# The 64-row matmul of the first feed-forward layer runs over 128 rows, with one more copy of weights

## The chip, the cores and the metric

The kernel runs on one core of a Trainium2 chip. The metric is the device time of one execution in microseconds (us), as the median over repeated runs. The names of the engines are those of the profile: PE is the matrix engine and PEld its weight loads, DVE, ACT and POOL are the vector, scalar and general engines, SP issues all transfers (DMA).

## The reference, cut to what matters

The program is a recurrent attention (mLSTM) followed by a feed-forward layer with a layer norm, over 4 batches, 8 heads of width 40, 768 time steps, all in float32:

```
attn_out = _attn_ref(q, k, v, i_gate, f_gate, o_gate)      # (4, 8, 768, 40)
x = attn_out.transpose(0, 2, 1, 3).reshape(4, 768, 320)
xn = (x - mean(x)) / sqrt(var(x) + 1e-6) * g_ln            # over the last axis
out = x + maximum(xn @ w_ch1, 0) @ w_ch2                   # w_ch1: 320 x 1280, w_ch2: 1280 x 320
```

The change touches only the product `xn @ w_ch1`. Its inner dimension is 320, that is 128 + 128 + 64.

## The kernel before

**Tiling.** Time is cut into 6 chunks of 128 steps; a step `st` of the attention is one chunk of one batch (24 steps). Two steps make a pair of 256 rows, and the feed-forward runs once for each pair (12 units `u`). In a unit the 1280 hidden columns are taken in 5 blocks `f` of 256, each in two halves `i` of 128.

**Precision in two parts.** The products of the feed-forward take operands of type `F32R`, so each operand is split into a high part and the small rest, and three of the four products of parts are summed: high by high, low weights by high data, high weights by low data. `w1h`, `w1l` are the parts of `w_ch1`, `XH`, `XL` those of the normalised rows, `hh`, `hl` those of the hidden values.

**The third slice of the inner dimension** has only 64 rows, and the other 64 partitions are put to use: in `XH[:, 2]` partitions 0 to 63 hold the high part of the last 64 features, and partitions 64 to 127 hold the low part of the same 64 features (`emit_xl`, L596, writes it there; the transposed input has these 64 features twice). `w1h[:, 2]` holds the high weights in both halves of the partitions, so a single matmul over 128 rows gives high by high and high by low. The product of low weights with high data takes partitions 0 to 63 alone, in a matmul over 64 rows.

**One half of the first layer**, `mm1` (task `m1`, L603 to L615), is thus eight matmuls that add up in one place: two `w1h` by `XH`, two `w1l` by `XH` over 128 rows, one `w1l` by `XH` over 64 rows, two `w1h` by `XL`, and one `w1h` by `XH` over 128 rows (third slice). There are 12 x 5 x 2 = 120 such halves. After both halves of a block ACT makes `hh` (L619) and DVE makes `hl` (L625), and `mm2` (L639 to L641, six matmuls for each of two halves of the rows) adds them into the second layer's output. `emit_ob` (L645) adds the residual, and a transfer stores the result.

**Weights.** They come in as raw float32 pairs, are converted by tasks `cA` to `cL`, and the key `"r"` is the third slice: the conversion (L671 to L717) fills partitions 0 to 63 for the columns 0 to 639 and partitions 64 to 127 for the columns 640 to 1279. `copy_r` (L722) then copies a half of the columns into the other half of the partitions by a transfer on SP: twice for `w1h`, and once for `w1l` (columns 640 to 1279 into partitions 0 to 63).

**Order.** All engines run a fixed order, written by a planner (`Plan`): each task has an engine, a duration, the tasks that it follows, buffers that it takes and gives, and a rank; the engine takes the ready task of least rank. The ranks come from a table of parameters (`TUNE`) and a table of offsets by task name (`OFF`, with `cR.0` -15.3, `cR.1` -10.4, `cR.2` -32.3). The planner prices `m1` at 0.87 us. What it leaves is one order of instructions per engine; on the chip an engine waits in that order. SP's transfers wait in order too, so that a transfer behind one that waits for a buffer is late with it.

Of the kernel before, what the change touches and what calls it, by code (L numbers as in the profile page):

```python
# [37 lines left out]


class Plan:  # L40
    """Orders the program: every engine takes, among the tasks that are ready, the one of least rank."""

    LAT = 0.12
    WIN, SLEEP, WAKE = 3.413, 0.45, 0.72
# [5 lines left out]
    def add(self, key, eng, us, fn, after=(), take=(), give=(), rank=0.0, kind=0, size=0, start=0.0, seq=None, load=1.0):  # L50
        rank += OFF.get(".".join(str(k) for k in key), 0.0)
        self.tasks[key] = dict(
            key=key, eng=eng, us=us, fn=fn, after=[a for a in after if a], take=take, give=give, rank=rank, kind=kind,
            size=size, start=start, seq=seq, load=load,
        )
# [95 lines left out]
def mlstm_moe_kernel(  # L151
# [40 lines left out]
    w1h = const.tile([128, 3, FF], F32R)  # L192
    w1l = const.tile([128, 3, FF], F32R)
# [409 lines left out]
    def mm1(p, f, i):  # L603
        if i == 0:
            h1_t[p, f] = ps_1.tile([128, 2, 256], F32, tag="h", name="h")
        ps = h1_t[p, f]
        XH, XL = XH_t[p], XL_t[p]
        cs = slice((2 * f + i) * 128, (2 * f + i + 1) * 128)
        ops = [(w1h[:, k, cs], XH[:, k]) for k in range(2)]
        ops += [(w1l[:, k, cs], XH[:, k]) for k in range(2)]  # L610
        ops += [(w1l[0:64, 2, cs], XH[0:64, 2])]
        ops += [(w1h[:, k, cs], XL[:, k]) for k in range(2)]
        ops += [(w1h[:, 2, cs], XH[:, 2])]
        for n, (a, x) in enumerate(ops):
            nc.tensor.matmul(ps[:, i], a, x, start=(n == 0), stop=(n == len(ops) - 1))  # L615
# [42 lines left out]
    def load_w(key):  # L658
        if key == "r":
            wload(key, w1r, 640)  # L660
        elif key[0] == "a":
            wload(key, w1a[key[1]], 512)
        else:
            wload(key, w2[key[1]], 640)

    def conv_a(key):
        n = 512 if key[0] == "a" else 640
        raw = w_st.pop(key)[:, :n].bitcast(I32).rearrange("p (n two) -> p n two", two=2)
        lo, hi = raw[:, :, 0], raw[:, :, 1]
        t = stage_p.tile([128, 640], I32, tag="t", name="wt")[:, :n]  # L670
        nc.scalar.activation(out=t.bitcast(F32), in_=hi.bitcast(F32), func=AF.Abs)  # L671
        w_st["t", key] = (lo, hi, t)

    def conv_x(key, e):
        t = w_st["t", key][2].bitcast(F32)
        e.tensor_scalar(out=t, in0=t, scalar1=UMIN, scalar2=None, op0=ALU.max)

    def conv_t(key, i):
        lo, hi, t = w_st["t", key]
        if i == 0:  # L680
            nc.vector.tensor_scalar(
                out=t, in0=t, scalar1=3, scalar2=0x3FFFFFF8, op0=ALU.logical_shift_left, op1=ALU.bitwise_and
            )
        elif i == 1:
            nc.vector.scalar_tensor_tensor(
                out=t, in0=hi, scalar=-0x40000000, in1=t, op0=ALU.bitwise_and, op1=ALU.bitwise_or
            )
        else:
            nc.vector.scalar_tensor_tensor(
                out=lo, in0=lo, scalar=29, in1=t, op0=ALU.logical_shift_right, op1=ALU.bitwise_or  # L690
            )
            w_st["t", key] = lo.bitcast(F32)
# [24 lines left out]
            e.tensor_tensor(out=l, in0=tf[ps], in1=h.bitcast(F32), op=ALU.subtract)  # L717

    def copy_r(i):
        w, a, h = ((w1h, 0, 0), (w1h, 1, 1), (w1l, 1, 1))[i]  # L720
        cs = slice(640 * h, 640 * h + 640)
        nc.sync.dma_start(  # L722
            out=w[64 - 64 * a:128 - 64 * a, 2, cs].bitcast(F32), in_=w[64 * a:64 * a + 64, 2, cs].bitcast(F32)
        )
# [135 lines left out]
    def plan_conv(n):  # L860
        key = keys[n]
        f = (n - 1) // 2
        r = TUNE["c0"] + n if n < 2 else T0 + TUNE["cv"] + TUNE["cs"] * (n - 2)
        rl = (TUNE["wl0"], TUNE["wl1"])[n] if n < 2 else TUNE["wl"] + TUNE["ws"] * (n - 2)
        k = 0.8 if key[0] == "a" else 1.0
        add(("wl", n), "sp", 0.5, lambda: load_w(key), [], seq=("wl", n - 1) if n else None, take=["wraw"], rank=rl,
            size=655360 * k, start=rl)
        xe, le = TUNE["cx"][n], TUNE["cl"][n]
        sc = le == "p"
        add(("cA", n), "act", 0.53 if key[0] == "a" else 0.64, lambda: conv_a(key), [("wl", n)], seq=("cA", n - 1) if n else None, take=["t"],  # L870
            rank=r, start=TUNE["cst"] if n > 1 else 0.0)
        add(("cX", n), "pool" if xe == "p" else "dve", (1.8 if xe == "p" else 0.41) * k,
            lambda: conv_x(key, nc.gpsimd if xe == "p" else nc.vector), [("cA", n)], rank=r)
        for i, d in enumerate((0.42, 0.75, 0.75) if key[0] != "a" else (0.35, 0.61, 0.61)):
            add(("cT", n, i), "dve", d, lambda i=i: conv_t(key, i), [("cT", n, i - 1) if i else ("cX", n)],
                give=["t"] if i == 2 else [], rank=r)
        if key == "r":
            dh, dl = 1.25, 3.0 if sc else 1.47
        elif key[0] == "a":
            dh, dl = 0.53, 1.24 if sc else 0.61  # L880
        else:
            dh, dl = 0.64, 1.5 if sc else 0.74
        add(("cH", n), "act", dh, lambda: conv_h(key), [("cT", n, 2)], rank=r)
        add(("cL", n), "pool" if sc else "dve", dl, lambda: conv_l(key, nc.gpsimd if sc else nc.vector), [("cH", n)],
            give=["wraw"], rank=r)
        if n == 0:
            for i in range(3):
                add(("cR", i), "sp", 0.6, lambda i=i: copy_r(i), [("cL", 0)], rank=r + i, size=163840)

    def plan_unit(u):  # L890
        r = slot(u)
        k = TUNE["k"] if u < 2 else KF // 2

        def before(u, f, m):
            last = KF // 2 - 1
            if u > 1 or TUNE["k"] > last:
                t = (u, f - 1) if f else (u - 1, last) if u else None
            else:
                ks = TUNE["k"]
                seq = [(v, g) for h in ((0, ks), (ks, last + 1)) for v in range(2) for g in range(*h)]  # L900
                i = seq.index((u, f))
                t = seq[i - 1] if i else None
            return (f"m{m}", *t, 1) if t else None

        def rank(f):
            if u > 1:
                return r + 4 * f
            if f < k:
                return T0 + TUNE["RA"] * u + 4 * f
            return T0 + TUNE["RB"] + 4 * (f - k) + 4 * u * (KF // 2 - k)  # L910

        for f in range(KF // 2):
            r = rank(f)
            for i in range(2):
                add(("m1", u, f, i), "pe", 0.87, lambda f=f, i=i: mm1(u, f, i),
                    [("xl", 2 * u), ("xl", 2 * u + 1), ("cL", 1 + 2 * f), ("cR", 0 if f < 2 else 2),
                     ("m1", u, f, 0) if i else before(u, f, 1) if k < 5 or f else None],
                    seq=("m1", u - 1, 4, 1) if u and k == 5 and not f and not i else None,
                    take=[] if i else ["h"], give=["xt"] if i and f == KF // 2 - 1 else [], rank=r + i)
            add(("hh", u, f), "act", 0.48, lambda f=f: emit_hh(u, f), [("m1", u, f, 1)], take=["ht"], rank=r)  # L920
            add(("hl", u, f), "dve", 0.61, lambda f=f: emit_hl(u, f), [("hh", u, f)], give=["h"], rank=r)
            for j in range(2):
                add(("m2", u, f, j), "pe", 0.81, lambda f=f, j=j: mm2(u, f, j, k),
                    [("hl", u, f), ("cL", 2 + 2 * f), ("m2", u, f - 1, j) if f and k == 5 else None, ("m2", u, f, 0) if j else before(u, f, 2) if k < 5 else None],
                    take=[f"o{j}"] if f in (0, k) else [], give=["ht"] if j else [], rank=r + 6 + j)
                if f in (k - 1, KF // 2 - 1):
                    add(("ob", u, j, f), "dve", 0.41, lambda j=j: emit_ob(u, j), [("m2", u, f, j)], give=[f"o{j}"],
                        rank=r + 4)
        for j in range(2):
            add(("out", u, j), "sp", 0.5, lambda j=j: store(u, j),  # L930
                [("ob", u, j, KF // 2 - 1), ("ob", u, j, k - 1) if k < KF // 2 else None], give=["y"], rank=slot(u),
                size=163840)
# [108 lines left out]
```

## Time and profile before

| what | us |
|---|---|
| runs (three) | 480.77, 483.7, 489.62 |
| median | 483.7 |
| span of the profiled execution | 477.9 |
| PE busy in it | 440.4 (92%) |
| DVE, ACT, POOL busy | 230.4, 176.2, 159.5 |

The page of the profile gives the profiled execution's span, from its first to its last instruction, and no other time of it; the fastest of the three runs is 2.9 us above the span, the median 5.8. A matmul's busy time in the profile runs from its start to a modelled end and overlaps the next one's, so the step from one matmul's start to the next one's is read from starts. The granted clock is the TensorE clock as a share of the higher of its two levels (2.4 and 1.2 GHz), as a mean over a stretch.

### The profile page before, as it was taken

To read this page: it belongs to the slowest core of one execution; us is meant where nothing else is said; L and a number is where in the kernel's file an instruction comes from. 1 tells how busy PE (TensorE), PEld (TensorE's weight loads), DVE (VectorE), ACT (ScalarE), POOL (GpSimd) and SP (SyncE) were. 2 spreads that over 40 slices of the span, in tenths; PEclk is the share of its full clock that TensorE was granted. 3 is DMA by queue.
4 is the path that set the end of the run, shared out by engine and by line. 5 is a ranking of instruction groups with operands and counts; after the bars stand their busy time and mean duration, and the time that the engine had idled before them with its cause. 6 is when DMAs were issued, how large, how long until landed. Compare 5 with 4: busy or idle time off the path is not lost.

```text
span 477.9 us, 7347 instructions
## 1 busy us (share of the span) xinstructions
PE 440.4 (92%) x2704; PEld 386.5 (81%) x2706; DVE 230.4 (48%) x524; ACT 176.2 (37%) x438; POOL 159.5 (33%) x195
## 2 busy tenths in 40 slices
PE   8999998999789997699998799988979988999996
PEld 4886787889679886688997698977868977989885
DVE  2475869975164752544545325453463443433321
ACT  3356556751151343414443313244243334222200
POOL 1145449661341560613623433252250522100100
PEclk8555779899979999579999859999997998999999
DMA  8935757637845879425776743686465585000000
GB/s 241 291 103 148 233 148 256 163 93 207 190 124 145 235 206 213 122 80 169 194 198 162 183 126 110 161 237 184 130 194 167 132 259 118 1 0 29 0 29 27
DMA packets 52721, 71.82 MB, mean 150 GB/s; under 512 B 3330, under 2 KB 45862, under 8 KB 52686
## 3 DMA queue, kind: packets, MB, share of 16 engines
q1 hardware_dynamic: 52686, 71.36, 54.1%
q8 instruction: 21, 0.34, 0.3%
q14 instruction: 14, 0.11, 0.1%
HBM read 46.83 MB, written 4.12 MB: 107 GB/s over the span
## 4 chain that ended last, share of the span: by engine, by line
PE 61%; DMA 22%; DVE 7%; SPq 3%; POOL 2%; issue 2%; ACT 2%; POOLq 0%; DVEq 0%; ACTq 0%
PE h L615 25%; DMA w<-gsc 8%; PE Y L481 6%; PE o L639 5%; PE s L411 5%; PE o L641 5%; PE o L640 5%; PE kv L444 2%; DMA og<-in_og_dram 2%; DMA raw<-in_qk_dram 2%; DMA ks<-raw 2%; DMA qs<-hi 2%; DMA qs<-raw 2%; SPq L257 2%; DMA eg<-esc 2%
## 5 line engine op out<-in xcount | busy, mean ns | idle before, releaser
L615 PE MATMUL h<-xh,w1h 128*128 128x256 f32 x360 | 91.2, 312 | 0.0
L615 PE MATMUL h<-xh,w1l 128*128 128x256 f32 x360 | 89.4, 327 | 0.0
L639 PE MATMUL o<-w2h,hh 128*128 128x320 f32 x240 | 83.1, 346 | 6.6 <-ACT hh L619 5.4
L619 ACT ACTIVATE hh<-h 128x512 fp32r<-128x512 f32 x60 | 35.6, 594 | 136.0 <-PE h L615 124.4
L641 PE MATMUL o<-w2h,hl 128*128 128x320 f32 x240 | 77.3, 322 | 0.5 <-DVE hl L625 0.5
L640 PE MATMUL o<-w2l,hh 128*128 128x320 f32 x240 | 76.8, 320 | 0.0
L615 PEld LDWEIGHTS h<-xh,w1l 128*128 128x128 f32 x360 | 62.8, 200 | 16.6 <-issue 2.5
L625 DVE SCALAR_TENSOR_TENSOR hl<-h,hh 128x512 fp32r<-128x512 f32 x60 | 41.2, 687 | 63.0 <-ACT hh L619 62.8
L363 ACT ACTIVATE w<-w,ar_sb 128x128 f32<-128x128 f32 x176 | 55.0, 390 | 33.1 <-POOL w L339 32.9
L615 PEld LDWEIGHTS h<-xh,w1h 128*128 128x128 f32 x360 | 64.3, 204 | 0.6
L615 PE MATMUL h<-xl,w1h 128*128 128x256 f32 x240 | 63.6, 348 | 0.0
L481 PEld LDWEIGHTS Y<-tok,w 128*128 128x128 f32 x384 | 55.4, 216 | 1.5 <-POOL rstd L552 1.1
L481 PE MATMUL Y<-tok,w 128*128 128x42 f32 x384 | 53.9, 293 | 0.6 <-ACT xh L584 0.6
L639 PEld LDWEIGHTS o<-w2h,hh 128*128 128x128 f32 x240 | 48.0, 200 | 7.5 <-ACT hh L619 5.8
L615 PEld LDWEIGHTS h<-xl,w1h 128*128 128x128 f32 x240 | 37.9, 199 | 16.4 <-issue 2.2
L641 PEld LDWEIGHTS o<-w2h,hl 128*128 128x128 f32 x240 | 47.6, 198 | 1.5 <-DVE hl L625 1.5
L418 DVE TENSOR_TENSOR w<-s,w 128x512 f32<-128x512 f32 x48 | 33.0, 688 | 31.4 <-PE s L411 26.5
L640 PEld LDWEIGHTS o<-w2l,hh 128*128 128x128 f32 x240 | 47.8, 199 | 0.0
L411 PE MATMUL s<-qs,ks 120*128 120x128 f32 (+1 forms) x240 | 41.0, 305 | 3.9 <-DMA qs<-raw 2.0
L411 PEld LDWEIGHTS s<-qs,ks 120*128 120x128 f32 (+1 forms) x240 | 36.2, 217 | 8.4 <-issue 7.5
L514 POOL TENSOR_TENSOR ogr<-og,rec 128x320 f32<-128x320 f32 x24 | 18.8, 781 | 65.3 <-DVE rec L507 50.1
L248 POOL TENSOR_TENSOR raw<-raw,hi 120x768 f32<-120x768 f32 x18 | 33.0, 1837 | 14.9 <-ACT hi L243 14.9
(91 smaller groups left out, 518.2 us busy)
## 6 DMA issues: line engine op xcount, KB each, us to landing
w<-gsc SPq DMA_DIRECT2D x22, 512.0 KB
tok<-in_tok_dram SPq DMA_DIRECT2D x12, 698.0 KB
raw<-in_qk_dram SPq DMA_DIRECT2D x9, 720.0 KB
ks<-hi SPq DMA_DIRECT2D x36, 180.0 KB
qs<-hi SPq DMA_DIRECT2D x36, 180.0 KB
out_dram<-y SPq DMA_DIRECT2D x24, 160.0 KB
qn<-in_qn_dram SPq DMA_DIRECT2D x10, 360.0 KB
eg<-esc SPq DMA_DIRECT2D x30, 120.0 KB
```

Source lines behind the costliest of these rows:

```text
L248: nc.gpsimd.tensor_tensor(out=raw[:, :, j], in0=raw[:, :, j], in1=hi[:, :, j], op=ALU.subtract)
L363: nc.scalar.activation(out=w[:, h], in_=w[:, h], func=AF.Exp, bias=ar_sb[:, c, 0, hb:hb + 1])
L411: nc.tensor.matmul(ps[:, hh], ks[:, h], qs[:, h], start=True, stop=True)
L418: nc.vector.tensor_tensor(out=w[:, half * 4:half * 4 + 4], in0=s_t.pop((st, half)), in1=w[:, half * 4:half * 4 + 4], op=ALU.mult)
L481: nc.tensor.matmul(Y[:, h * VA:(h + 1) * VA], w[:, h], tok_t[p][:, j, h * VA:(h + 1) * VA], start=(c == 0), stop=(c == 0 or h == H - 1), s ...
L514: nc.gpsimd.tensor_tensor(out=ogr, in0=og_t[c][:, b].rearrange("p (h d) -> p h d", h=H), in1=rec.to_broadcast([128, H, D]), op=ALU.mult,)
L615: nc.tensor.matmul(ps[:, i], a, x, start=(n == 0), stop=(n == len(ops) - 1))
L619: nc.scalar.activation(out=hh, in_=h1_t[p, f], func=AF.Relu)
L625: nc.vector.scalar_tensor_tensor(out=hl.rearrange("p a t -> p (a t)"), in0=ps.rearrange("p a t -> p (a t)"), scalar=0.0, in1=hh.rearrange( ...
L639: nc.tensor.matmul(ps, hh[:, i, sl], w2h[:, ff], start=(ff in (0, 2 * cut)), stop=False)
L640: nc.tensor.matmul(ps, hh[:, i, sl], w2l[:, ff], start=False, stop=False)
L641: nc.tensor.matmul(ps, hl[:, i, sl], w2h[:, ff], start=False, stop=(ff in (2 * cut - 1, KF - 1)))
```

## The change

In `mm1` the fifth of the eight matmuls takes all 128 partitions of `w1l[:, 2]` and `XH[:, 2]` in place of partitions 0 to 63; it then adds the product of low weights and low data for the last 64 features too. For this `w1l[:, 2]` must hold the low weights in both halves of the partitions for all columns, so `copy_r` gets a fourth copy (`w1l`, columns 0 to 639, into partitions 64 to 127), and the copies are numbered anew. An `m1` task now names copy 1 or 3 (the `w1l` copy of its columns) as what it follows, where it named copy 0 or 2. The docstring of `Plan` is gone.

```diff
-        ops += [(w1l[0:64, 2, cs], XH[0:64, 2])]
+        ops += [(w1l[:, 2, cs], XH[:, 2])]
...
     def copy_r(i):
-        w, a, h = ((w1h, 0, 0), (w1h, 1, 1), (w1l, 1, 1))[i]
+        w, a, h = ((w1h, 0, 0), (w1l, 0, 0), (w1h, 1, 1), (w1l, 1, 1))[i]
...
-            for i in range(3):
+            for i in range(4):
                 add(("cR", i), "sp", 0.6, lambda i=i: copy_r(i), [("cL", 0)], rank=r + i, size=163840)
...
                 add(("m1", u, f, i), "pe", 0.87, lambda f=f, i=i: mm1(u, f, i),
-                    [("xl", 2 * u), ("xl", 2 * u + 1), ("cL", 1 + 2 * f), ("cR", 0 if f < 2 else 2),
+                    [("xl", 2 * u), ("xl", 2 * u + 1), ("cL", 1 + 2 * f), ("cR", 1 if f < 2 else 3),
```

## Rows read from the trace of the kernel before

**Rows 1.** The page: the span, the engines' busy time, and the shares of the chain that ended last.
```profile
span 477.9 us, 7347 instructions
...
PE 440.4 (92%) x2704; PEld 386.5 (81%) x2706; DVE 230.4 (48%) x524; ACT 176.2 (37%) x438; POOL 159.5 (33%) x195
...
PE 61%; DMA 22%; DVE 7%; SPq 3%; POOL 2%; issue 2%; ACT 2%; POOLq 0%; DVEq 0%; ACTq 0%
```

**Rows 2.** Busy time by stretch: the stretch, its length, busy time (and instructions) of each engine, the mean granted clock, the busy share of the DMA engines, GB/s. Three stretches from the first feed-forward matmul to the end, then the conversion of the weights.
```profile
53.00:90.00 37.00, 35.38 (x194) 31.17 (x193) 30.10 (x52) 21.97 (x50) 24.14 (x20) 0.77 0.66 191
90.00:396.00 306.00, 278.88 (x1800) 250.41 (x1799) 145.43 (x347) 111.11 (x277) 110.80 (x133) 0.92 0.63 169
396.00:477.90 81.90, 76.86 (x507) 68.43 (x505) 26.43 (x63) 17.48 (x44) 7.04 (x13) 0.99 0.09 27
...
65.00:90.00 25.00, 23.38 (x154) 21.54 (x153) 23.20 (x37) 17.57 (x42) 20.40 (x18) 0.90 0.67 200
```

**Rows 3.** The chain that ended last, by line, in the stretches 53 to 90, 90 to 396 and 396 to 478 us (the view cuts each line off at its end).
```profile
by line: PE h L615 27.2%; DVE wraw L689 8.1%; issue 5.6%; DVE wt L681 5.1%; PE Y L481 4.6%; PE Y L432 4.2%; PE o L639 4.1%; DVE wt L685 3.8%; PE o L640 3.7%; PE o L641 3.7%; DVE hl L625 3.5%; PE kv L444 3.4%; DVE w1l L717 3.2%; DVE xn L563 
...
by line: PE h L615 24.9%; DMA w<-gsc 12.6%; PE o L639 5.3%; PE Y L481 4.8%; PE o L641 4.6%; PE o L640 4.5%; PE s L411 3.6%; DMA og<-in_og_dram 3.3%; DMA raw<-in_qk_dram 3.1%; DMA ks<-raw 2.8%; DMA qs<-hi 2.8%; DMA qs<-raw 2.7%; SPq L257 2.7
...
by line: PE h L615 42.4%; PE o L639 10.3%; PE o L641 10.3%; PE o L640 9.8%; DMA out_dram<-y 8.9%; PE Y L481 6.0%; PE Y L432 2.6%; PE xT L578 1.6%; DVE y L645 1.2%; PE s L411 1.0%; DVE hl L625 0.9%; ACT hh L619 0.7%; DVE y L523 0.6%; issue 0
```

**Rows 4.** Groups of instructions by line and shape, of the matmuls and weight loads that take `w1l`, over 128 and over 64 rows: busy us, mean ns of one, idle time before.
```profile
L615 PE MATMUL h<-xh,w1l 128*128 128x256 f32 x240 | 50.0, 291 | 0.0
...
L615 PE MATMUL h<-xh,w1l 64*128 64x256 f32 x120 | 47.9, 399 | 0.0
...
L615 PEld LDWEIGHTS h<-xh,w1l 128*128 128x128 f32 x240 | 39.7, 203 | 0.0
...
L615 PEld LDWEIGHTS h<-xh,w1l 64*128 64x128 f32 x120 | 23.1, 193 | 16.6 <-issue 2.5 <-ACT wt L671 0.2
```

**Rows 5.** Instructions in order of time, of one half at the full clock (448.70 to 450.04) and the start of the next: start us, length us, engine, line; neighbours of one kind stand merged (x2, x3) or alone, by the window that was asked for, and come from several windows here. "64*128" is the 64-row matmul or load.
```profile
448.70 0.29 PE L615 MATMUL h<-xh,w1h 128*128 128x256 f32 x1
...
448.82 0.28 PE L615 MATMUL h<-xh,w1h 128*128 128x256 f32 x1
448.94 0.40 PE L615 MATMUL h<-xh,w1l 128*128 128x256 f32 x2
...
448.95 0.19 PEld L615 LDWEIGHTS h<-xh,w1l 128*128 128x128 f32 x1
...
449.06 0.59 PE L615 MATMUL h<-xh,w1l 128*128 128x256 f32 x2
449.27 0.18 PEld L615 LDWEIGHTS h<-xh,w1l 64*128 64x128 f32 x1
...
449.27 0.38 PE L615 MATMUL h<-xh,w1l 64*128 64x256 f32 x1
449.58 0.39 PE L615 MATMUL h<-xl,w1h 128*128 128x256 f32 x1
...
449.80 0.28 PE L615 MATMUL h<-xl,w1h 128*128 128x256 f32 x1
...
449.92 0.52 PE L615 MATMUL h<-xh,w1h 128*128 128x256 f32 x3
450.28 0.70 PE L615 MATMUL h<-xh,w1l 128*128 128x256 f32 x3
```

**Rows 6.** The same view of one half at half the clock (205.31 to 207.75), with the weight load of its 64-row matmul.
```profile
205.31 0.77 PE L615 MATMUL h<-xh,w1h 128*128 128x256 f32 x2
205.88 1.14 PE L615 MATMUL h<-xh,w1l 128*128 128x256 f32 x3
206.95 0.80 PE L615 MATMUL h<-xl,w1h 128*128 128x256 f32 x2
207.54 0.41 PE L615 MATMUL h<-xh,w1h 128*128 128x256 f32 x1
207.75 0.41 PE L444 MATMUL kv<-tok,kp 128*120 128x126 f32 x1
...
206.44 0.28 PEld L615 LDWEIGHTS h<-xh,w1l 64*128 64x128 f32 x1 [0.22 <-issue]
```

**Rows 7.** The same view where a half follows a transposition over 32 rows (`gT`), at the full clock.
```profile
299.12 0.24 PE L310 MATMUL gT<-id_sb,uu 32*128 32x32 f32 x1
299.29 0.50 PE L615 MATMUL h<-xh,w1h 128*128 128x256 f32 x2
```

**Rows 8.** A transfer on the chain that ended last (start us, length us, what), and the busy time (columns as in the first view by stretch above) around it.
```profile
117.02 11.90 DMA w<-gsc
...
117.00:131.00 14.00, 11.68 (x83) 10.43 (x82) 2.77 (x9) 1.74 (x7) 4.10 (x5) 1.00 0.85 201
```

**Rows 9.** Who waited for whom: waiting engine and line, for what, us in total, times, longest us (SP's own queue); and, in order of time, a matmul with the idle time before it and what ended that in brackets.
```profile
SPq L211 <- DMA qs<-raw: 7.1, 4, 2.3
...
133.37 0.63 PE L639 MATMUL o<-w2h,hh 128*128 128x320 f32 x1 [4.68 <-ACT hh L619]
```

**Rows 10.** SP's queue around the copies: start us, length us, line, what.
```profile
26.80 0.57 SPq L722 DMA_DIRECT2D w1l<-w1l  x1
...
28.05 1.13 SPq L722 DMA_DIRECT2D w1h<-w1h  x2
38.29 0.33 SPq L216 DMA_DIRECT2D tok<-in_tok_dram  x1
```

## The prediction

> **What bounds the kernel now.** I read the page first. PE is busy in 92% of the span and no other engine in half of it; the chain that ended last lies 61% on PE and 22% on transfers [rows 1]. An average over stages with different limits doesn't say what a PE saving is worth, so next came the busy time by stretch [rows 2]. Up to 53 us there is no feed-forward matmul. From 53 to 90 us the weights are converted, and in its later part DVE is busy in 23.20 of 25 us. From 90 to 396 us PE is busy in 278.9 of 306 us, and 0.63 of the DMA engines' time is taken. From 396 us on the transfers are nearly over (0.09), and PE has 76.9 of 81.9 us. Then the chain by the same stretches [rows 3]: the line of the first layer, L615, holds 27.2% of it in the first, 24.9% in the middle and 42.4% at the end. The reader is to see that the changed line is the largest part of the chain everywhere, but that in the middle transfers stand between its pieces.
>
> Last I looked at what the 64-row matmul costs. By the groups, a 64-row matmul lasts 399 ns and a 128-row one of the same operands 291 ns [rows 4], but ends are modelled and overlap, so the price is read from starts. In one half at the full clock [rows 5] the eight matmuls start at 448.70, 448.82, 448.94, 449.06, 449.27, 449.58, 449.80 and 449.92; from 449.92 to 450.28, the third start of the next half, lie three steps, 0.12 each. So the steps are 0.12, 0.12, 0.12, **0.21, 0.31, 0.22**, 0.12, 0.12: 1.34 us. The three long ones lie before the 64-row matmul, after it, and after the next. The weight loads say why: an ordinary load starts with the matmul ahead of it (449.06's at 448.95, beside the one of 448.94), while the 64-row matmul's load starts at 449.27, only with its own matmul. The array goes from 128 rows to 64 and back with nothing loaded in advance, and the step behind catches up. The same catching up is seen after another change of rows: behind a 32-row transposition the first two matmuls of a half take 0.50 us [rows 7], like the two `xl` ones here (449.58 to 449.80 plus a length of 0.28), where a half in plain order has 0.40.
>
> **The change part by part.** (1) With 128 rows all eight should step by 0.12. That saves 0.21 + 0.31 + 0.22 - 3 x 0.12 = **0.38 us for each half** at the full clock. At half the clock [rows 6] the plain step is 0.21 (207.54 to 207.75); from the third to the fifth start 0.56, to the sixth 0.51, to the eighth 0.59, so the long steps are 0.35, 0.51 and 0.38, and 0.61 us goes of 2.44. Bounds: if the third gap belongs to reading `XL` and stays, 0.28 remains; I take 0.38, since [rows 7] shows that gap without `XL`.
>
> (2) How much of it shortens the end? 120 halves save about 48 us of PE's time (120 x 0.38, and 0.23 more for the ten or so at half clock). On the chain alone: at the end 42.4% of 81.9 us is 34.7 us, 26 halves, **9.8 us**. In the middle 24.9% of 306 us is 76.2 us; a granted clock of 0.92 means that 0.16 of the time is at half, so 0.84 x 0.284 + 0.16 x 0.25 = 0.279 of it goes, **21.2 us** (about 50 halves). In the first stretch 10.1 us, of which 2.5 would go; I take nothing, because behind it DVE converts weights almost without pause and the next matmuls wait for those. The other 39 or so halves run beside transfers of the chain, as in the 11.90 us of `w` from 117.02, when DMA is 0.85 busy and moves 201 GB/s [rows 8]. Such a transfer isn't shortened by a faster PE, so there some 15 us become PE's wait.
>
> (3) The fourth copy. SP's issues of the three copies take 0.57 and 1.13 for two [rows 10]; a fourth is 0.57 us, its wait is the one that the first copy has already ended, and behind it stands the `tok` load, which isn't issued until 38.29. So nothing is delayed; the first feed-forward matmul is at 53. Without that cover it would cost 0.57 us and about 0.8 us for 160 KB (an estimate, at 201 GB/s). The copy that the first blocks now follow is issued over 20 us ahead of them. SP's transfers wait on a ring of earlier ones, which shifts by one; such waits are up to 2.3 us [rows 9]. Bounds 0 to 2.3, taken as 0.
>
> (4) The planner. It prices `m1` the same, so ranks move only for the copies: the offsets of `cR.0` to `cR.2` now meet other copies and `cR.3` has none. A pick elsewhere could flip through the copy's 0.6 us of SP time. No row prices that; the nearest is PE's wait of 4.68 us [rows 9], so up to 5 us either way, taken as 0, because SP stands waiting right behind the copies. The matmul reads more partitions, and those are written by the same tasks as before.
>
> (5) The sum: 9.8 + 21.2 = 31 us. The profiled span becomes 477.9 - 31 = 447. What lies around the span isn't listed; the fastest run is 2.9 and the median 5.8 us above it, which gives 450 to 453. **I forecast 451 us.** Of the middle, what is late next are the transfers and the waits behind them (`w`, then ACT's `hh`, before which PE stood 4.68 us).
>
> A rule against it: a 64-row load lasts 193 ns and a 128-row one 203 [rows 4]. The Trainium skill, TensorE: Matmul & The Clock Gate, section LDWEIGHTS (loading the stationary operand), says that a load over 32 rows takes as long as one over 128, as only columns count; the trace agrees. By that rule alone the rows matter nowhere and the sum is 0.
>
> **The rivals.** A, the forecast, 443 to 462 us: the chain's share is saved, with an error of some 10 us for its clock and its transfers. 0.62.
>
> B, all of PE's time is saved: the order holds work back behind PE so that transfers start earlier too and hide again. 48 us go: 436, and to 430 if denser matmuls also bring the clock back sooner from half, of which the middle has 0.16 x 306 = 49 us. For it: SP's loads wait for PE's results. Against: DMA at 0.85 of its time on the chain. 0.17.
>
> C, the middle is held by transfers and by the clock. Only the end's 9.8 us are sure. If the wait in the middle grows from 27 us (306 - 278.9) by 15 and half-clock time with it, from 49 to 76 us, 13.6 us are given back: 465. If half the middle's saving is lost, 462. Together 462 to 474. 0.13.
>
> D, the change doesn't do what it says: the long steps stay with 128 rows, because they come from the place and not from the rows: 484, 478 to 488 with the bounds above. Against it is [rows 5]: the third slice's `w1h` matmul over 128 rows (449.92 + 0.12) has plain steps on both sides. The trace shows a 128-row load beside a 128-row matmul (448.95). The same page of the Trainium skill, under Part 3, What overlaps and what doesn't, says that loads overlap a matmul in flight only where the row groups differ; by that rule the new load couldn't run ahead and the time would be this one, but the load at 448.95 speaks against it. 0.04.
>
> E, slower. PE stands idle, then the clock is at half, as at 133.37 behind the wait of 4.68 us (0.63 us for a matmul that has some 0.31 otherwise). With PE ahead of the transfers there are more such waits. Each us at half costs about 0.5; to be 2% above 483.7 the clock must eat 31 + 10 us, 82 us more at half, so the middle's granted clock would fall from 0.92 to about 0.8. That gives 493. Against it: a half that starts at half clock has 8 x 0.21 of 2.44 us in plain steps and would have all of it, so PE is denser just when it has work. 0.04.
>
> **How the numbers follow.** The forecast is A's, 451 us. The range takes A whole, most of B and the near part of C: 433 to 466. 2% of 483.7 is 9.7 us, about what a measurement of this kernel tells from no change (its three runs spread over 8.9). Faster is A, B and C: 0.92. Same is D: 0.04. Slower is E: 0.04.
>
> **What would show it.** In the changed profile L615 has no 64-row form, and the starts in a half step by 0.12 throughout, 0.96 in all; the pair of `xl` takes 0.40. Four copies stand at SP before 30 us. The stretch from the last large transfers to the end is some 10 us shorter, the middle some 21, while PE's idle time there grows from 27 to about 40 us and L615's share of the chain falls below a quarter. The forecast is wrong if the long steps are still there (D), if the middle doesn't shorten though they are gone (C), or if the granted clock of the middle leaves 0.92 by more than 0.05 either way.

## The result, and the profile after

| | before | changed | ratio (95% interval) |
|---|---|---|---|
| as first measured, 4 runs each | 482.24 us | 463.38 us | 0.9641 (0.9538 to 0.9745) |
| again, 11 and 6 runs | 488.05 us | 464.74 us | 0.9636 (0.9571 to 0.9700) |
| profiled span | 477.9 us | 459.9 us | |

The ratios compare, of each kernel's runs beside each other, those within 1.5% of its fastest; the medians take in all of its runs. By the ratios the change takes 17 us off, by the medians 19 to 23, where 31 were forecast; the two profiled spans are 18.0 apart. The kernel before spreads over 471 to 498 us in the runs of this study, the changed one over 461 to 467. The page after, against [rows 1]: PE's busy time and its share are down, and transfers have a larger part of the chain.

```profile
span 459.9 us, 7356 instructions
...
PE 404.9 (88%) x2704; PEld 381.1 (83%) x2706; DVE 230.1 (50%) x524; ACT 176.1 (38%) x438; POOL 158.8 (35%) x195
...
PE 57%; DMA 26%; DVE 7%; SPq 4%; issue 2%; POOL 2%; ACT 1%; POOLq 0%; DVEq 0%; ACTq 0%
```

The groups by shape, against [rows 4]: there is no 64-row form left, and a `w1l` matmul lasts 296 ns throughout.

```profile
L615 PE MATMUL h<-xh,w1l 128*128 128x256 f32 x360 | 66.5, 296 | 1.0 <-ACT w L363 0.8 <-DVE w1l L717 0.3
```

Two halves in order of time at the full clock, against [rows 5]:

```profile
435.28 0.51 PE L615 MATMUL h<-xh,w1l 128*128 128x256 f32 x3
435.63 0.40 PE L615 MATMUL h<-xl,w1h 128*128 128x256 f32 x2
435.86 0.52 PE L615 MATMUL h<-xh,w1h 128*128 128x256 f32 x3
436.21 0.54 PE L615 MATMUL h<-xh,w1l 128*128 128x256 f32 x3
```

From the first `w1l` matmul of one half to that of the next it is 0.93 us (435.28 to 436.21), where it was 1.34: 0.41 us saved, against 0.38 forecast. The three `w1l` take 0.35 to the next start, and the `xl` pair is at 0.40. So the step itself did all that it was to do, 120 times. The order of the matmuls, and of everything on DVE, ACT and POOL, is that of before, and SP's differs only in the copies:

```profile
27.05 0.49 SPq L722 DMA_DIRECT2D w1h<-w1h  x1
27.60 1.23 SPq L722 DMA_DIRECT2D w1l<-w1l  x2
38.13 0.33 SPq L216 DMA_DIRECT2D tok<-in_tok_dram  x1
```

The `tok` load behind the copies is issued at 38.13 (38.29 before) [rows 10]: the fourth copy is hidden.

**Where the rest went.** As the order is the same, the same instruction can be looked up in both traces. Here are the starts of four, before and after, in order of time: the first product of step 4, a matmul of the first layer at the forecast's border of 90 us, a transposition, and a matmul of the first layer at its border of 396 us:

```profile
79.22 1.04 PE L411 MATMUL s<-qs,ks 40*128 40x128 f32 x7
89.95 0.37 PE L615 MATMUL h<-xh,w1h 128*128 128x256 f32 x1
119.55 0.49 PE L578 MATMUL xT<-id_sb,xn 128*128 128x128 f32 x3
395.81 0.63 PE L615 MATMUL h<-xh,w1l 128*128 128x256 f32 x2
```

```profile
79.60 2.04 PE L411 MATMUL s<-qs,ks 40*128 40x128 f32 x8 [6.68 <-DMA ks<-in_q_dram]
93.56 0.56 PE L615 MATMUL h<-xh,w1h 128*128 128x256 f32 x1
124.00 0.49 PE L578 MATMUL xT<-id_sb,xn 128*128 128x128 f32 x3
389.44 0.63 PE L615 MATMUL h<-xh,w1l 128*128 128x256 f32 x2
```

Up to the second of them the changed kernel is 3.6 us behind (93.56 for 89.95). From there to the fourth, the forecast's middle, it gains 10.0 us (305.86 to 295.88), and from there to the end 11.6 (82.1 to 70.5). Together that is the 18.0 us between the spans.

The first products of step 4 start at nearly the same time in both (79.22, 79.60): PE, done sooner with the first halves, waits 6.68 us for a load of `ks`. SP issued this load 5.3 us sooner than before, but it took 11.35 us to land, where before it was there within 5.8 (73.39 to 79.22) and PE didn't wait for it. The load's issue before, then its issue after, the load on the chain that ended last, and the ten us that it shares with other transfers (columns as in [rows 2]; the DMA engines are busy in 0.96 of them):

```profile
73.39 0.31 SPq L237 DMA_DIRECT2D ks<-in_q_dram  x1
...
68.11 0.32 SPq L237 DMA_DIRECT2D ks<-in_q_dram  x1
68.11 11.35 DMA ks<-in_q_dram
68.00:78.00 10.00, 4.26 (x29) 3.54 (x28) 5.31 (x11) 3.98 (x13) 5.93 (x5) 0.95 0.96 271
```

From the products to the transposition the changed kernel loses 4.1 us (40.33 to 44.40). The granted clock by stretch shows why, and what the middle lacks (columns as in [rows 2]), before and then after:

```profile
83.00:107.00 24.00, 23.62 (x151) 21.00 (x150) 20.79 (x40) 16.77 (x43) 16.95 (x20) 0.93 0.50 135
89.95:395.81 305.86, 278.74 (x1800) 250.27 (x1799) 145.29 (x347) 110.92 (x277) 110.80 (x133) 0.92 0.63 169
```

```profile
77.00:104.00 27.00, 24.40 (x102) 22.86 (x103) 17.08 (x34) 15.26 (x36) 13.36 (x15) 0.50 0.40 118
93.56:389.44 295.88, 256.75 (x1800) 248.80 (x1798) 146.47 (x345) 111.30 (x277) 111.42 (x134) 0.87 0.66 175
```

Behind the wait PE works at 0.50, where it had 0.93: it does 102 matmuls in 27 us, the last 2.6 us of the wait included, where before it did 151 in 24. The middle holds the same 1800 matmuls in both. PE's idle time in it grew from 27.1 to 39.1 us, and its time at half the clock from 49 to 74 us; 25 us more at half cost some 12. The middle has 83 of the 120 halves, at 0.41 us some 34 us. Less 12 for the waits and 12 for the clock, 10 are left, and 10.0 were measured.

These two terms vary from one execution to the next. In the profiles of the changed kernel run again and of the rows alone (both below), the same stretch has 46.8 and 35.4 us of idle time and 74 and 81 us at half.

### The profile page after: what moved, and what is told of

It is laid out like the page before. It is cut to its first block, busy times and chain, and to the rows that moved or that the text cites. A ratio compares the mean times of both kernels' runs of the same rounds, so it can differ in the third digit from the quotient of the medians.

```text
span 459.9 us, 7356 instructions
## 1 busy us (share of the span) xinstructions
PE 404.9 (88%) x2704; PEld 381.1 (83%) x2706; DVE 230.1 (50%) x524; ACT 176.1 (38%) x438; POOL 158.8 (35%) x195
## 4 chain that ended last, share of the span: by engine, by line
PE 57%; DMA 26%; DVE 7%; SPq 4%; issue 2%; POOL 2%; ACT 1%; POOLq 0%; DVEq 0%; ACTq 0%
PE h L615 19%; PE s L411 7%; DMA eg<-esc 7%; PE Y L481 7%; PE o L639 5%; PE o L641 5%; PE o L640 5%; DMA out_dram<-y 4%; DMA ks<-in_q_dram 3%; DMA tok<-in_tok_dram 3%; DMA w<-gsc 3%; SPq L257 2%; PE kv L444 2%; DMA qs<-raw 2%; DMA raw<-in_qk_dram 2%; PE Y L432 2%
## 5 line engine op out<-in xcount | busy, mean ns | idle before, releaser
L639 PE MATMUL o<-w2h,hh 128*128 128x320 f32 x240 | 84.2, 351 | 12.0 <-ACT hh L619 12.0
L615 PE MATMUL h<-xh,w1l 128*128 128x256 f32 x360 | 66.5, 296 | 1.0 <-ACT w L363 0.8
L481 PEld LDWEIGHTS Y<-tok,w 128*128 128x128 f32 x384 | 58.8, 228 | 1.6 <-POOL rstd L552 1.1
L481 PE MATMUL Y<-tok,w 128*128 128x42 f32 x384 | 57.2, 304 | 0.5 <-ACT xh L584 0.5
L615 PEld LDWEIGHTS h<-xh,w1l 128*128 128x128 f32 x360 | 55.7, 206 | 1.4 <-issue 0.9
L411 PE MATMUL s<-qs,ks 120*128 120x128 f32 (+1 forms) x240 | 44.6, 326 | 11.9 <-DMA ks<-in_q_dram 7.2
L411 PEld LDWEIGHTS s<-qs,ks 120*128 120x128 f32 (+1 forms) x240 | 39.4, 236 | 16.6 <-issue 9.2
L615 PE MATMUL h<-xl,w1h 128*128 128x256 f32 x240 | 50.1, 292 | 0.0
L615 PEld LDWEIGHTS h<-xl,w1h 128*128 128x128 f32 x240 | 39.8, 204 | 0.0
```

The lines of the kernel that those rows point to most:

```text
L411: nc.tensor.matmul(ps[:, hh], ks[:, h], qs[:, h], start=True, stop=True)
L481: nc.tensor.matmul(Y[:, h * VA:(h + 1) * VA], w[:, h], tok_t[p][:, j, h * VA:(h + 1) * VA], start=(c == 0), stop=(c == 0 or h == H - 1), s ...
L639: nc.tensor.matmul(ps, hh[:, i, sl], w2h[:, ff], start=(ff in (0, 2 * cut)), stop=False)
```

## The experiments

The times are medians beside runs of the kernel before on the same chip. Kernels of one set share these: 481.39 us (first set, four kernels), 488.05 (second, four), 486.73 (third, three), 487.49 (the last). The sets ran on different chips; the changed kernel itself ran in the second one alone, so where it is compared with a kernel of another set, the ratios to the kernel before are the safer measure.

### Is it the rows, and what does the copy cost?

**The copy alone.** The 64-row matmul is put back into the changed kernel.

```diff
-        ops += [(w1l[:, 2, cs], XH[:, 2])]
+        ops += [(w1l[0:64, 2, cs], XH[0:64, 2])]
```

> The changed kernel with the 64-row matmul put back: what is left of the change is the fourth copy, the new numbers of the copies and what the first layer's tasks follow. Theory (copy free): the time of before, 482 us, within 1%, steps of 0.21, 0.31 and 0.22 us as in before, and the loads of ks and qs that PE waited for at 79.6 us in the changed kernel issued at 73 us as in before. Rival (the copy or the shifted ring of SP's transfers costs what the forecast missed, some 13 us): 490 to 495 us.

486.55 us, ratio 1.0036 (0.9914 to 1.0158): no cost that can be told from none (the interval reaches 1.6% up and 0.9% down, some 8 and 4 us). But its profiled run, of 488.48 us, had a span of 486.7 us, 8.8 above the profile of before, and nearly all of that arose between the first products of step 4 (79.11 us) and the transposition (128.18; before 79.22 and 119.55); at the end the two are as far apart as there. In that stretch the clock was at 0.51 (before: 0.93), and in the profile of two small matmuls in a row, below, at 0.50 (second line):

```profile
83.00:107.00 24.00, 24.00 (x95) 21.09 (x95) 17.19 (x30) 11.63 (x27) 15.11 (x17) 0.51 0.36 95
...
83.00:107.00 24.00, 24.00 (x97) 21.53 (x96) 16.70 (x29) 12.03 (x28) 14.91 (x16) 0.50 0.39 96
```

So the clock can fall behind step 4's load with the long steps still there, too. In the profile on which the forecast stood it hadn't, but for 3.4 us. Against this profile the changed kernel's span is 26.8 us shorter (486.7 - 459.9), near the forecast's 31; that is one pair of profiles, and the runs say 17 to 23.

**The rows alone**, without the copy:

```diff
-        ops += [(w1l[0:64, 2, cs], XH[0:64, 2])]
+        ops += [(w1h[:, 2, cs], XH[:, 2])]
```

> The kernel before, its fifth matmul over 128 rows with the high weights w1h in place of the low ones (the product of low weights and high data of the last 64 features is left out and that of the high parts counted twice): the rows alone, no fourth copy. Theory: the time of the changed kernel, 463 us, within 1%, steps of 0.12 us. Rival (the copy costs 13 us): about 450 us.

464.38 us, as the changed kernel (463.38, 464.74), and its steps around the fifth matmul are plain ones. Its ratio is 0.9804 (0.9618 to 0.9989), nearer to 1 than the changed kernel's 0.964, as the kernel before had its fastest runs in this set (471.31 to 478.19 us). So the copy costs nothing and gives nothing that the runs can show, and the rows are the effect.

**Two small matmuls in a row.**

```diff
-        ops += [(w1l[0:64, 2, cs], XH[0:64, 2])]
+        ops += [(w1l[0:64, 2, cs], XH[0:64, 2])] * 2
```

> The kernel before with the 64-row matmul issued twice in a row (its product is counted twice). Theory (each change between 128 and 64 rows costs, the small matmul itself doesn't): the second one steps by 0.12 us behind the first, a half takes 1.46 us, and the time rises by 120 x 0.12 = 14 us at most, to about 490 to 496 us. Rival (a small matmul is slow in itself): the second costs as much as the first, 0.5 us a half, 60 us in all, up to 540 us.

497.49 us, ratio 1.0462 (1.0272 to 1.0653). In order of time, of this kernel:

```profile
442.09 0.40 PE L615 MATMUL h<-xh,w1h 128*128 128x256 f32 x2
442.32 0.39 PE L615 MATMUL h<-xh,w1l 128*128 128x256 f32 x2
442.64 0.38 PE L615 MATMUL h<-xh,w1l 64*128 64x256 f32 x1
442.86 0.27 PE L615 MATMUL h<-xh,w1l 64*128 64x256 f32 x1
443.06 0.50 PE L615 MATMUL h<-xl,w1h 128*128 128x256 f32 x2
443.40 0.28 PE L615 MATMUL h<-xh,w1h 128*128 128x256 f32 x1
443.52 0.31 PE L639 MATMUL o<-w2h,hh 128*128 128x320 f32 x1
```

A half takes 1.43 us (442.09 to 443.52), 0.09 more than the half of [rows 5] with one small matmul, and the medians below say 0.11: the second one adds about a plain step. The theory's sum held, its step didn't. The second small matmul starts 0.22 us behind the first (442.64 to 442.86) and not 0.12; in return the step behind it, back to 128 rows, is 0.20 (442.86 to 443.06) and not 0.31. The 16 us of the median are a little over the theory's 14, but the interval holds both. In sum the price lies in going to 64 rows and back, not in each small matmul. The Trainium skill, TensorEngine Tiling (Array Packing), section Key Properties, says that a change of the tiling mode drains the engine while a change of tile doesn't. The traces fit that with 0.38 to 0.41 us for a pair of changes at the full clock; what the engine does in that time they don't show.

**Two small matmuls apart**, the second ahead of the `w1l` ones:

```diff
+        ops += [(w1l[0:64, 2, cs], XH[0:64, 2])]
         ops += [(w1l[:, k, cs], XH[:, k]) for k in range(2)]
```

> The kernel before with a second 64-row matmul apart from the first, between the w1h and the w1l matmuls of a half (its product is counted twice). Theory (each pair of changes of rows costs 0.38 us beside the plain step of 0.12): 0.50 us for each of 120 halves, 60 us of PE's time, and since PE then hides the transfers all the better nearly all of it is in the end: 530 to 545 us. Rival (a small matmul costs the same wherever it stands): the same time as with the two in a row.

529.09 us by the median, 48 us above before, just under what the theory gave. The four runs spread over 509.93 to 538.79, so the time alone says little; the steps say more. From the last matmul ahead of the first small one (471.00) to the last of the half (472.61):

```profile
471.00 0.28 PE L616 MATMUL h<-xh,w1h 128*128 128x256 f32 x1
471.21 0.38 PE L616 MATMUL h<-xh,w1l 64*128 64x256 f32 x1
471.52 0.51 PE L616 MATMUL h<-xh,w1l 128*128 128x256 f32 x2
471.96 0.38 PE L616 MATMUL h<-xh,w1l 64*128 64x256 f32 x1
472.26 0.50 PE L616 MATMUL h<-xl,w1h 128*128 128x256 f32 x2
472.61 0.28 PE L616 MATMUL h<-xh,w1h 128*128 128x256 f32 x1
```

These seven steps take 1.61 us, 0.77 more than seven plain ones: each small matmul brings the same 0.38. Over all halves that ran at the full clock, from a half's first matmul to the next start on PE, the medians are 1.38 us before, 0.97 in the changed kernel and in the one with the rows alone, 1.49 with two small ones in a row and 1.89 with two apart. So place and pairs of changes decide: 0.51 us for the second pair, as the theory had it, 0.11 for a second small matmul in a row. Of the 61 us that this adds to PE's time, 48 are in the median's end.

### Is PE still what sets the time?

> The changed kernel as it is, to stand beside the three others of this set: 463 us. In its trace PE waits some 7 us before the first product of queries and keys of step 4 (at 72 to 80 us), and the clock is at half from there to about 104 us.

464.74 us. In its profile the wait for `ks` is 4.1 us long and not 7, and the stretch 77 to 104 us is at 0.50 again.

**The fifth matmul left out**, from the changed kernel:

```diff
-        ops += [(w1l[:, 2, cs], XH[:, 2])]
```

> The changed kernel without the fifth matmul (the product of low weights and high data of the last 64 features is left out): another 0.12 us less in each of 120 halves, 14 us of PE's time. Theory (the middle is held by the chain's transfers as well): the end's 29 halves and about half of the others count, 6 to 9 us: 454 to 457 us. Rival (PE alone sets the time, and the forecast's 31 us fell short for another reason): 14 us, 449 us.

462.70 us, 2 us less. 14 us of PE's time, of which 3.5 in the last 29 halves, are all but given back; this is less than the theory gave, and the rival's 449 is far off. The chain in the middle of this kernel (104 to 400 us), second line, has 9.0% on the first layer, where the changed kernel's has 16.9%, first line, and that of before had 24.9% [rows 3] (the view cuts the first line off):

```profile
by line: PE h L615 16.9%; DMA eg<-esc 10.3%; DMA out_dram<-y 5.9%; PE Y L481 5.8%; PE o L639 4.9%; PE o L641 4.3%; DMA tok<-in_tok_dram 4.3%; PE o L640 4.3%; DMA w<-gsc 4.0%; SPq L257 3.6%; DMA qs<-raw 3.5%; DMA raw<-in_qk_dram 3.2%; PE s L
...
by line: DMA w<-gsc 10.5%; DMA out_dram<-y 10.0%; PE h L614 9.0%; DMA eg<-esc 7.9%; DMA og<-in_og_dram 6.3%; issue 5.9%; PE Y L481 4.9%; SPq L257 4.5%; DMA qs<-hi 3.4%; DMA raw<-in_qk_dram 3.3%; PE o L638 2.8%; PE o L640 2.6%; SPq L324 2.5%
```

But PE waits no longer for it. From the same transposition as above to a product of the state near the end of the middle, the changed kernel run again (first line) and this one (second line) have:

```profile
122.34:401.44 279.10, 229.95 (x1641) 222.44 (x1638) 127.14 (x307) 98.95 (x244) 99.36 (x118) 0.89 0.66 175
121.42:398.79 277.37, 230.96 (x1565) 223.17 (x1562) 128.98 (x307) 99.54 (x244) 99.32 (x118) 0.86 0.66 176
```

PE's idle time is 49.2 us and then 46.4, but its time at half the clock goes from 61 to 79 us. In this pair of profiles the left-out matmuls came back as a lower clock, with 76 matmuls fewer in the stretch and the same busy time.

**Half the size of `w`'s transfers**, in the changed kernel and in the one before:

```diff
-            out=w, in_=gsc[c:c + 1].rearrange("o (h b) t -> o h b t", b=B)[:, :, b].to_broadcast([128, H, C])
+            out=w[:, 0:4],
+            in_=gsc[c:c + 1].rearrange("o (h b) t -> o h b t", b=B)[:, 0:4, b].to_broadcast([128, 4, C])
...
-            out=w, in_=w, pattern=[[0, H], [1, C]], compare_op
+            out=w[:, 0:4], in_=w[:, 0:4], pattern=[[0, 4], [1, C]], compare_op
...
-            nc.scalar.activation(out=w[:, h], in_=w[:, h], func=AF.Exp
+            nc.scalar.activation(out=w[:, h], in_=w[:, h % 4], func=AF.Exp
```

> The changed kernel with the 22 transfers of w at half their size, 256 KB each (four of the eight heads; POOL's selection runs on four, and the other four heads' exponentials read the first four's, so these heads' weights are left out). PE's work is the same. Theory (with the long steps gone, transfers and what waits for them hold the middle): PE's waits before o L639 (for hh, behind w on ACT) shrink and the time falls by 5 to 12 us, to 452 to 460 us. Rival (PE still sets the time): 462 to 465 us.

> The same edit on the kernel before. Theory (there PE sets the time more than the transfers do): less falls than in the changed kernel, 0 to 5 us, within the spread of its runs. Rival (transfers held the middle in the same way before the change): the same 5 to 12 us.

450.36 us, ratio 0.921 (0.9098 to 0.9322), and 468.65 us, ratio 0.9666 (0.9579 to 0.9753). The kernel before gains 18 us by the medians and 16 by the ratio; the changed kernel gains 14 by the medians, and some 20 by the ratios (0.9636 to 0.921). That is more than the theory gave for either, and for the kernel before the theory fell: it gains about as much, as the rival had it. PE and the transfers were both in the chain before the change, one after the other, as the chain had said (61% and 22%), and not one in the other's shadow. With the small transfers the change is worth 18.3 us by the medians (468.65 - 450.36) and 22 by the ratios, no less than with the full ones.

**Both**, half the size of `w`'s transfers and no fifth matmul, by the two edits above:

> The changed kernel with w's transfers at half size (as in the run with half w, which took 450 us) and without the fifth matmul of each half (as in the run that left it out, which took 463 us, 2 us under the changed kernel). Theory (the transfers of w were what kept the 14 us of the left-out matmuls from counting): now 6 to 10 us of them count, 440 to 445 us. Rival (below this amount of matmuls something else than w's transfers holds the middle, the order of SP's queue or the clock): 447 to 451 us.

442.05 us (439.93 to 443.76), 8.3 us below the median of 450.36 with the matmul in, within what the theory gave. But those four runs spread over 443.08 to 455.08 us: against the faster two of them (443.08, 448.43) it is 4 us, and the two profiled spans are 441.3 and 441.0. So it isn't shown that `w`'s transfers kept the left-out matmuls from counting. The two profiles point to the rival's other cause, the clock. Between the same two instructions as above, with the matmul in and then without it:

```profile
116.19:377.92 261.73, 225.32 (x1641) 219.62 (x1638) 126.34 (x307) 99.49 (x246) 91.70 (x118) 0.90 0.63 171
117.90:379.91 262.01, 226.16 (x1565) 219.92 (x1563) 127.40 (x306) 98.81 (x244) 91.98 (x118) 0.87 0.62 170
```

PE's idle time is the same (36.4 and 35.9 us), and the time at half rises from 51 to 68 us. As with the full transfers, what was left out came back at half the clock.

### The load and the clock at 72 to 104 us

**The load earlier**: step 4's queries and keys are issued before the weights for which SP waits.

```diff
+        seq = [k for k, _ in self.order]
+        seq.remove(("stk", 4))
+        seq.insert(seq.index(("wl", 8)), ("stk", 4))
+        for k in seq:
+            if tasks[k]["fn"]:
+                tasks[k]["fn"]()
```

(The tasks' functions are called from here, after the planner has run, and no longer within it.)

> The changed kernel with one transfer pair moved in SP's order: the queries and keys of step 4 are issued ahead of the load of weights that SP waits for at 49 to 55 us, not behind four later loads at 68 us. Theory (the stretch up to 106 us is set by this load and by the half clock behind the wait for it): the wait of 7 us goes, the clock stays up or falls for a shorter time, and the time is 450 to 457 us. Rival (PE then waits for the next thing at the same place, such as the converted weights): 461 to 465 us.

460.53 us, ratio 0.9485 (0.9418 to 0.9551): 4 us below the changed kernel by the medians, 7 by the ratios (0.9636 there), which is the upper edge of what the theory gave. Its runs spread over 455 to 467, and its profile is of the longest, 467.43. In it the wait for `ks` is gone, but PE waits 2.7 us for converted weights in that stretch, and 77 to 104 us are at 0.62.

**The wait filled** with matmuls of zeros into the tile that the products will overwrite:

```diff
+        for _ in range(28 if st == 4 and not half else 0):
+            nc.tensor.matmul(
+                ps.rearrange("p a t -> p (a t)"), wu_bf[:, :C], wu_bf, start=True, stop=True, skip_group_check=True
+            )
```

> The changed kernel with 28 matmuls of zeros, 512 columns each, ahead of the first product of step 4, some 6 us at the full clock, in place of the wait there; nothing else is moved. Theory (the wait costs mostly through the clock, which falls in it and stays at half for 27 us): the clock stays at full in most of 77 to 104 us and the time is 450 to 457 us. Rival (the clock falls for the matmuls behind the wait, which fill few columns, not for the wait): half clock there as before, 463 us or a few more.

458.95 us, ratio 0.952 (0.9477 to 0.9564), 6 us below the changed kernel of the same set. PE in order of time, and then the stretch 77 to 104 us (columns as in [rows 2]), of this kernel:

```profile
74.87 5.99 PE L410 MATMUL s<-wu_bf 128*128 128x512 bf16 x27
80.79 1.16 PE L415 MATMUL s<-qs,ks 40*128 40x128 f32 x8
...
77.00:104.00 27.00, 26.19 (x185) 22.38 (x184) 23.38 (x46) 20.09 (x50) 17.94 (x20) 1.00 0.48 141
```

The products start no earlier than before (80.79, after 79.60), but the granted clock is 1.00 in place of 0.50, and PE does 185 matmuls in the stretch, 18 of them fillers, in place of 102. So in this profile the matmuls behind the wait didn't bring the clock down by themselves. Over the six runs of each the span's granted clock is 0.888 on the mean, and 0.863 without the filling; that isn't all due to the filling, as this profile has 0.95 in its first 53 us, ahead of any filler, where the changed kernel's has 0.65. In the profile the transposition comes at 115.03, 9.0 us ahead of the changed kernel's, and the last matmul only 3.7 ahead (452.47, 456.18): the middle's clock is 0.87, and PE waits there for the same things.

**Both**, the early load and 14 such matmuls:

> The changed kernel with both, the early load of step 4's queries and keys and 14 matmuls of zeros ahead of its first product. Theory (what counts is the clock in 77 to 104 us, and the wait left by the early load is shorter than 7 us): full clock there with 3 us of filling in place of 6, 453 to 458 us, at or below the 459 us of filling alone. Rival (the fillers are too few to keep the clock, or later waits take the gain): 459 to 463 us.

455.70 us, ratio 0.9371 (0.929 to 0.9452): the best version that computes all of it, some 9 us below the changed kernel of the other set, 31 below the kernel before, and within what the theory gave. In its profile the stretch 77 to 104 us is at 0.94.

## Why the prediction was right or wrong

The direction, the cause and the range held (463.4 within 433 to 466). The size was off, 17 to 23 us for 31, and the time lies 1.4 us outside A's stretch and in C's: the range held by the near part of C that it had taken in.

(1) The saving for a half: 0.38 forecast, 0.41 seen, with all three gaps gone. That the third one is catching up and not `XL` was right.

(2) The middle's share is the term that was mis-sized. By the forecast's own borders (90 and 396 us), the first stretch was taken at 0 and lost 3.6 us, the middle was forecast at 21.2 and gave 10.0, and the end was forecast at 9.8 and gave 11.6 (it has 29 halves, where the chain had told of 26). What failed in the middle is the clock: the sum took it to stay at 0.92, and it was at 0.87, with 49 us at half before and 74 after, some 12 us lost. The waits were foreseen: some 15 us of the saving were to become PE's wait, outside the 21.2, and PE's idle time grew by 12.0.

In the first stretch I took 0, because DVE's conversion would hold the next matmuls. Up to 79 us that was right (-0.4), for a reason that I hadn't named: what held PE was a load of `ks` that was issued sooner and took 11.35 us to land among other transfers. Behind it the clock fell to half, for 27 us, where the profile of before has 3.4, and 3.2 us more were lost up to the border (10.73 to 13.96). The run with the copy alone and that with two small matmuls in a row show that this fall comes with the long steps too, in some runs; the profile that I took all durations from was one without it. With the copy alone the forecast's middle has 69 us at half, not 49. So a part of what I put down to the clock lies in the profile that the forecast started from, and how large a part stays open.

(3) and (4) The copy and the planner's picks at 0: right as far as the runs can tell, by the run of the copy alone, that of the rows alone, and the unchanged order.

(5) In the sum, the 3 to 6 us around the span were 1.8 in the changed kernel's profiled run (461.7 us, span 459.9). The rivals: C named the mechanism and nearly its numbers. It had PE's idle time in the middle grow from 27 us by 15 and the time at half from 49 to 76; measured were 39.1 and 74. C's 462 to 474 holds the time; it had a chance of 0.13. B failed: where SP issued a load sooner (`ks`, by 5.3 us) it landed no sooner in the profile after. D fell with the steps, and with it, for loads of 128 rows one behind the other, the rule of the Trainium skill's page TensorE: Matmul & The Clock Gate, Part 3, What overlaps and what doesn't. E did not come.

What stays open: which of the transfers sets the middle once `w`'s are small, whether fewer matmuls bring the clock down there or only met it, and why the clock falls in some runs of the same order of work and not in others. Before the fall in the run with the copy alone PE was idle for hardly longer than in the profile of before (1.3 and 1.2 us between 53 and 82.8), so a long wait is one way to it and not the only one.

## What to carry to other kernels

A matmul over fewer rows among full ones costs the change of rows twice, and the busy times of the profile hide that; the steps from start to start show it, and padding the operand with data that is already there can pay for itself. Value a PE saving by the chain, then take off what a less busy PE can lose through the clock. Compare two profiles between the same instructions, not between the same times. A filler in a wait that is known can pay though the wait stays.

## What was not expected of the hardware

The second of two 64-row matmuls in a row adds about 0.1 us, though a pair of changes costs 0.4; yet its own step is 0.22 us, and it is the step behind it that shrinks. A wait of 6.68 us was followed by 27 us at half the clock, and filling it with zeros kept 1.00 there: 6 us of the time for 6 us of work without a result. 120 matmuls left out, 14 us of PE's time, moved the median by 2 us, and the clock's time at half rose by 17 us in one stretch of the profile. And the same order of matmuls has the stretch from 83 to 107 us at 0.93 in one execution and at 0.51 in another.
